# Attention and two expert layers on one core: the zero fill in three pieces, tokens counted ahead of a hidden group, half of a weight load behind a branch

## The chip, the cores and the metric

The kernel runs on one core of a Trainium2 chip. The metric is the device time of one execution in microseconds (us); the median over several runs counts. Besides, one execution is recorded by the profiler; the rows below are from that one.

## What is computed

Three stages follow one another, all in float32, here cut to what matters:

```python
scores = np.matmul(q, k.transpose(0, 1, 3, 2)) / np.sqrt(D)        # B=2, H=8, S=576, D=64
kth = np.partition(scores, -32, axis=-1)[..., -32:-31]
scores = np.where(scores >= kth, scores, -1e9)                     # the 32 largest of each row
x = softmax(scores) @ v                                            # as 1152 tokens of 512 numbers

expert_idx = np.argmax(x @ w_gate, axis=1)                         # first layer: 8 experts, one per token
...                                                                # at most 288 tokens of an expert are kept
x[i] = gate_w[i] * (relu(x[i] @ w1[e]) @ w2[e])                    # w1[e]: 512x1024, w2[e]: 1024x512
...                                                                # second layer: the same without a limit
```

## The kernel before

**Attention.** 16 heads are taken in pairs: 8 units of 9 score tiles, 72 steps in all. A tile of 128 queries by 576 keys is multiplied on TensorE (PE), its top 32 are found on VectorE (DVE) with MAX8 and MATCH_REPLACE8, ScalarE (ACT) and GpSimd (POOL) make the mask, PE transposes the masked weights and multiplies by the values. Beside the tiles there are side jobs: loads, splits, transposes of later units, writes of finished x to DRAM, and fills. A table written by hand, `at(i, f)`, says at which step a job is issued; `run_jobs` issues the jobs of a step. SyncE (SP) has no work of its own: it issues DMAs in program order and waits where one needs data.

**Fills.** `tables(zero)` returns the set-up jobs; its last five are the parts of `fill(part)` (lines 172 to 184). Parts 0 to 2 zero a third of the output each, part 3 zeroes the tails of x and y, part 4 the rows of y behind the tiles (128 rows of 9x513 words; `nov[0] + 1` is 9). The steps are in the tuple `(15, 16, 24, 33, 46)` that is zipped with them. y is the DRAM tensor between the two expert layers.

**The picked expert.** Near the end of the attention the kernel picks the expert that then has most tokens (`early_jobs`) and loads its weights as `w_early` (`w1c`, 8 loads of 512 KB, step 60). A tile of 128 of its tokens (`blank`) can so be computed before the tokens are sorted. Its hidden layer has 8 groups of 128 units; the groups f=0 and 1 are done at the end of the attention (L1029, relus in L1031), the others in `early_hidden(f)` (L1848), four float32 products each, which the profile shows as eight records. `early_out(d)` (L1857) is the second layer of this tile, four groups d of eight products (16 records).

**Two branches.** `repair(trips)` (L1069) recomputes rows whose top 32 were cut short; `spill()` (L1657, L1659) computes blocks of an expert's tokens that exceed its tiles, as many as `nblk` says. All engines load the number and branch; neither body runs here.

**Start of the first expert layer**, `begin()`: `choose` (one-hot `oh` of each token's expert, L1531, DVE), `early_hidden(2)`, `count` (L1536 to L1541, PE: positions of tokens within their expert), hidden groups 3 to 7, `spin(9, 64)` (nine products that nobody reads, L124), `ranking` (DVE), `weights(0, 0)` (both halves of the first expert's w1, L1244, on SP), `assign` (`places`, L1588, PE; `early_out(0)`; gates, `gidx`, `nblk`, DVE), gathers of token rows (`bring`, L1233, POOL), `spill`, the casts of the loaded weights (L1285 on ACT, L1286 on DVE), w2 from ACT's queue (L1256), `early_out(1)` and `(2)`, transposes of the gathered rows (L1315, PE), then the first expert's layer 1 (L1358 and on).

In `begin()` the order of the calls is the order of the instructions on each engine:

```python
choose(0, nch)
early_hidden(2)
count(0, nch)
...
early_hidden(7, 0, KD // 2)
spin(9, 64)
weave(*ranking())
weights(0, 0)
assign()
```

Of the kernel before, what the change touches and what calls it, by code (L numbers as in the profile page):

```python
# [10 lines left out]
F32 = mybir.dt.float32  # L11
# [23 lines left out]
NCOL = len(COLS[0])  # L35
FAR = 5000.0
AWAY = 2048.0
RW = 513
# [16 lines left out]
def attn_moe_moe_kernel(ctx, tc, q, k, v, g1, w11, w12, capacity, g2, w21, w22, out):  # L55
    nc = tc.nc
# [3 lines left out]
    KD = Dm // 128  # L60
    KF = F // 128
# [56 lines left out]
    part = consts.tile([128, 1], F32)  # L118
# [15 lines left out]
    def tables(zero):  # L134
        def first():
            nc.gpsimd.iota(iot, pattern=[[1, 128]], base=0, channel_multiplier=0, allow_small_or_imprecise_dtypes=True)
            nc.gpsimd.iota(part, pattern=[[0, 1]], base=0, channel_multiplier=1, allow_small_or_imprecise_dtypes=True)
            nc.gpsimd.memset(wgh, 0.0)

        def gate_in(hh):  # L140
            nc.gpsimd.tensor_copy(wgh[hh * D:(hh + 1) * D, :, hh, :], wg[hh * D:(hh + 1) * D, 0])

        def rank_tables(part):
            for t_, cols, sizes in zip(tab, COLS, SIZES):
                for a, (r, t, m) in enumerate(cols):
                    if r >= 0 and t == 0 and r // 2 == part:
                        nc.gpsimd.memset(t_[:, 0, r:r + 1], float(a + 1))
                        nc.gpsimd.memset(t_[:, 1, r:r + 1], float(sizes[r]) - AWAY)

        def clear():  # L150
            nc.gpsimd.memset(lg1, 0.0)
            nc.gpsimd.memset(lg2, 0.0)
            nc.gpsimd.memset(revm[1], 0.0)
            nc.gpsimd.memset(code[1], 0.0)

        def order():
            nc.gpsimd.tensor_scalar(chosen, negid, AWAY, 1.0, op0=OP.mult, op1=OP.mult)
            nc.gpsimd.tensor_scalar(rev, iot[:, :E], -1.0, float(E), op0=OP.mult, op1=OP.add)
            nc.gpsimd.iota(tok1, pattern=[[128, NC]], base=1, channel_multiplier=1, allow_small_or_imprecise_dtypes=True)

        def order_all():
            nc.gpsimd.tensor_copy(revm[0], rev[:, None, :].to_broadcast([128, B * NC, E]))
            nc.gpsimd.tensor_scalar(code[0][:, 0], part.to_broadcast([128, B * NC]), 1.0, 64.0, op0=OP.mult, op1=OP.add)

        def tokens(b):
            for c in range(NC):
                nc.gpsimd.memset(code[0][:, 1, b * NC + c:b * NC + c + 1], b * S + c * 128 - 64)
            t = b * NC + NC - 1
            nc.gpsimd.memset(revm[0][TAIL:, t, :], -1.0)
            nc.gpsimd.memset(code[0][TAIL:, :, t], 0.0)  # L170

        def fill(part):
            n = N // 128 // 3
            if part < 3:
                nc.sync.dma_start(out[part * n * 128:(part + 1) * n * 128].rearrange("(n p) w -> p n w", p=128),
                                  zero[:, None, :Dm].to_broadcast([128, n, Dm]))
            elif part == 3:
                nc.sync.dma_start(x_d[N:, :], zero[:128 - TAIL, :Dm])
                for a, (r, t, m) in enumerate(COLS[0]):
                    if m < 128:  # L180
                        nc.sync.dma_start(y_d[a * 128 + m:(a + 1) * 128, :], zero[:128 - m, :RW])
            else:
                nc.sync.dma_start(y_d[(NCOL - 1) * 128:, :].rearrange("(n p) w -> p n w", p=128),
                                  zero[:, None, :RW].to_broadcast([128, nov[0] + 1, RW]))

        setup_ranks.extend(lambda k=k: rank_tables(k) for k in range(4))
        return [first, lambda: gate_in(0), lambda: gate_in(1), clear, order, order_all,
                lambda: tokens(0), lambda: tokens(1)] + [lambda k=k: fill(k) for k in range(5)]

    def attention():  # L190
        HP = H // 2
# [8 lines left out]
        with tc.tile_pool(name="ald", bufs=2) as ld, tc.tile_pool(name="awk", bufs=2) as wk, \  # L200
# [644 lines left out]
                    at(i0 + NT + 6 + d, normed, u, *w)  # L845
            at(1, load, 2, ("v",))
            at(1, setup[3])
            for i, f in zip((62, 63, 64, 66, 26, 28, 30, 32), setup_ranks + setup[4:-5]):
                at(i, f)
            early_ops, weights_in, found, turn_rows = early_jobs()  # L850
            behind = []
# [4 lines left out]
            at(60, weights_in)  # L856
            at(63, found)
            at(67, turn_rows)
            for i, f in zip((15, 16, 24, 33, 46), setup[-5:]):
                at(i, f)  # L860
            at(1, lambda: nc.gpsimd.memset(flv, -1.0))
            at(0, v_first)
# [164 lines left out]
            for f, o in enumerate((rest[:, 0, :128], side[:, 0, :128])):  # L1027
# [2 lines left out]
                                     start=(d == 0), stop=(d == KD - 1))  # L1030
                relus.append(lambda f=f, o=o: nc.scalar.activation(h_early[f].bitcast(F32), o, AF.Relu))  # L1031
            relus[0]()
            g = wk.tile([128, NC, 2, E], F32, name="g")
            for c0, c1 in ((0, M - 1), (M, NC)):
                shape = [128, c1 - c0, 2, E]
# [16 lines left out]
                nc.vector.scalar_tensor_tensor(l, last[:, hh, D:D + E], r3[:, hh:hh + 1], l, op0=OP.mult, op1=OP.add)  # L1052
            b, p = divmod(u, HP)
            xn = wk.tile([128, 2, D], F32, name="xn3", bufs=1)
            for hh in range(2):
                nc.scalar.activation(xn[:, hh], last[:, hh, :D], AF.Copy, scale=r3[:, hh:hh + 1])
            relus[1]()
            nc.sync.dma_start(x_d[b * S + (M - 1) * 128:b * S + M * 128, p * 128:(p + 1) * 128],
                              xn.rearrange("s h d -> s (h d)"))
            return trips  # L1060
# [114 lines left out]
    def moe(i, pools, src, lg, w1, w2, limit):  # L1175
# [5 lines left out]
        with ExitStack():  # L1181
# [410 lines left out]
            def assign(a=0):  # L1592
# [7 lines left out]
                if i == 0:  # L1600
                    nc.scalar.activation(cnt, pos[:, nch], AF.Copy)
                    nc.scalar.activation(poss, pos[:, :nch], AF.Copy)
                    early_hidden(7, KD // 2)
                    yTs[-1] = wk.tile([128, KD, ny], F32, name="yT")
                    early_out(0, 0, KF)
                for f in gates[:3] if i == 0 else gates:
                    f()
                nc.vector.tensor_copy(lowp, pi[:, :NCOL])
# [231 lines left out]
            def early_hidden(f, d0=0, d1=KD):  # L1840
                if f == 2:
                    hTs[-1] = wt.tile([128, KF, 1, 128], F32R, name="w2c", bufs=12)
                if d0 == 0:
                    early_ps["h"] = ps.tile([128, 512], F32, name="pp", bufs=4)
                ph = early_ps["h"]
                w_, k = piece(w_early[0], f)
                for d in range(d0, d1):
                    nc.tensor.matmul(ph[:, :128], w_[:, d, k * 128:(k + 1) * 128], rows0[:, d], start=(d == 0), stop=(d == KD - 1))  # L1848
                if d1 == KD:
                    hidden(hTs[-1], f, 128, ph[:, :128], False)  # L1850
# [29 lines left out]
            def begin():  # L1880
                bank()
                choose(0, nch)
                early_hidden(2)
                count(0, nch)
                nc.scalar.activation(dl, dl, AF.Exp)
                none = new([128, 1], "none", U32)
# [1 line left out]
                yr = wk.tile([128, RW], F32, name="yr", bufs=3)  # L1888
                gather(yr[:16, :Dm], none[:16])
                two.prepare()  # L1890
                for f in range(3, 7):
                    early_hidden(f)
                early_hidden(7, 0, KD // 2)
                spin(9, 64)
                weave(*ranking())
                weights(0, 0)
                assign()
                for j in range(2):
                    bring(j)
                for f in table["later"]:  # L1900
                    f()
                spill()
                early_gate()
                for t in range(len(tiles_of(1))):
                    bring(first[1] + t)
# [3 lines left out]
                weights(0, 1, eng=ACT)  # L1909
                for f in first_split[2:4]:  # L1910
                    f()
                early_out(1, 0, KF)
                early_out(2, 0, KF)
                xTs[0] = wk.tile([128, KD, 2, MOST], F32R, name="xT")
                q0, q1 = tiles_of(0)
                rows_in(0, *q0)
# [230 lines left out]
```

## Time and profile before

| | |
|---|---|
| median of 3 runs | 584.73 us (584.01, 587.02, 584.73) |
| the profiled execution | 584.83 us, span 583.2 us, mean granted clock of PE 0.998 |
| busy share of the span | PE 97%, DVE 82%, ACT 72%, POOL 46% |
| DMA moved | 100.76 MB, mean 173 GB/s |

How to read it: the span goes from the first to the last instruction. PE is busy nearly all the time by its records, but they are pipelined and their ends are modelled; a row's duration is longer than the distance of two starts. The shares are averages over two stages, attention (to about 250 us) and expert layers (the rest), which have different limits. "Idle before" in brackets behind a row is how long the engine stood still ahead of it and what released it; "issue" means that the profile shows nothing that it waited for. An engine name with a q (SPq, PEldq) is its sequencer, which issues DMAs, waits and branches.

### The profile page before, as it was taken

The page shows a single profiled execution, that of the slowest core. Times are in us where ns is not written, and L with a number is a line of the kernel's source. Part 1 is how long each engine was busy: PE and PEld are TensorE (multiplying, and loading weights), DVE is VectorE, ACT ScalarE, POOL GpSimd, SP SyncE. Part 2 cuts the span into 40 slices and gives each one's busy share as a digit, 9 for nine tenths or more (in the row PEclk, how much of TensorE's full clock was granted, in tenths as well). Part 3 has the DMA queues.
Part 4 walks back from the last instruction along what each step waited for, and adds up shares of the span by engine and source line. Part 5 has one row for each costly group of instructions (what it writes and reads, how often), then busy time and mean ns, then how long its engine had stood idle before and what let it go on. Part 6 is the DMA issues. An engine that isn't in the chain of part 4 may idle for free.

```text
span 583.2 us, 13992 instructions
## 1 busy us (share of the span) xinstructions
PE 566.5 (97%) x4786; PEld 539.4 (92%) x4786; DVE 475.9 (82%) x1588; ACT 419.3 (72%) x1040; POOL 266.4 (46%) x600
## 2 busy tenths in 40 slices
PE   8999999999999999989999999999999999999994
PEld 5799999999998999889999999998998899999993
DVE  6999999999999999868788778552588788889650
ACT  6789998999898978627687787552365677878650
POOL 8758888988897798546320111010103302220010
PEclk9999999999999999999999999999999999999999
DMA  6630513161291083055988768876777867678650
GB/s 146 142 83 2 169 46 114 44 127 43 75 149 25 1 246 85 22 175 198 341 278 289 231 204 259 276 220 229 228 252 234 288 227 263 231 243 298 213 204 14
DMA packets 85168, 100.76 MB, mean 173 GB/s; under 512 B 33925, under 2 KB 46725, under 8 KB 85088
## 3 DMA queue, kind: packets, MB, share of 16 engines
q1 hardware_dynamic: 79104, 86.69, 49.1%
q0 software_dynamic: 3728, 10.70, 5.2%
q10 hardware_dynamic: 2256, 2.39, 1.3%
q8 instruction: 40, 0.66, 0.5%
q14 instruction: 40, 0.33, 0.2%
HBM read 86.51 MB, written 13.74 MB: 172 GB/s over the span
## 4 chain that ended last, share of the span: by engine, by line
PE 36%; DMA 10%; issue 6%; DVE 2%; POOL 1%; ACT 1%; POOLq 0%; DVEq 0%; ACTq 0%
DMA out_dram<-yr,sidx 8%; PE pp L1365 8%; PE pp L1404 7%; PE pp L1351 3%; PE pp L1367 3%; PE pp L1406 3%; PE pl L1418 2%; PE pt L1315 1%; DMA xr<-x,gidx 1%; PE pt L1455 1%; PE pp L1400 1%; PE pp L1402 1%; PE pp L1401 1%; DMA xr<-y,gid 1%; PE pp L1354 1%
## 5 line engine op out<-in xcount | busy, mean ns | idle before, releaser
L622 PE MATMUL xb<-vx,pT 128*128 128x73 f32 (+1 forms) x800 | 94.0, 266 | 0.2 <-ACT pT L1012 0.2
L1365 PE MATMUL pp<-xT,w1c 128*128 128x352 f32 (+4 forms) x316 | 92.4, 361 | 0.4 <-DVE xT L1321 0.4
L1286 DVE TENSOR_TENSOR w2c<-raw,w2c 128x512 fp32r<-128x512 f32 x112 | 74.6, 684 | 18.9 <-ACT w2c L1285 17.4
L622 PEld LDWEIGHTS xb<-vx,pT 128*128 128x128 f32 (+1 forms) x800 | 87.1, 181 | 2.5 <-issue 1.3
L1404 PE MATMUL pp<-hT,w2c 128*128 128x416 f32 (+4 forms) x320 | 88.7, 356 | 0.1
L1406 PE MATMUL pp<-hT,w2c 128*128 128x208 f32 (+4 forms) x320 | 77.8, 243 | 0.0
L1367 PE MATMUL pp<-xT,w1c 128*128 128x176 f32 (+4 forms) x316 | 77.0, 244 | 0.0
L1285 ACT ACTIVATE w2c<-raw 128x512 fp32r<-128x512 f32 x112 | 67.4, 624 | 8.8 <-DMA raw<-in_moe_w_dram 5.1
L601 PE MATMUL pt<-ident,shifted 128*128 128x128 f32 x350 | 67.4, 278 | 0.0
L602 PE MATMUL pt<-negid,under 128*128 128x128 bf16 x350 | 63.5, 219 | 0.5 <-ACT under L592 0.5
L1286 DVE TENSOR_TENSOR w1c<-raw,w1c 128x512 fp32r<-128x512 f32 x88 | 56.0, 686 | 9.3 <-ACT w1c L1285 7.4
L1337 ACT ACTIVATE t<-pp 128x208 f32<-128x208 f32 (+4 forms) x120 | 37.5, 313 | 34.5 <-PE pp L1367 21.2
L1406 PEld LDWEIGHTS pp<-hT,w2c 128*128 128x128 f32 x320 | 61.0, 191 | 0.0
L1404 PEld LDWEIGHTS pp<-hT,w2c 128*128 128x128 f32 x320 | 60.0, 188 | 1.0 <-DVE hT L1331 0.8
L1365 PEld LDWEIGHTS pp<-xT,w1c 128*128 128x128 f32 x316 | 59.4, 188 | 1.4 <-DVE xT L1321 0.8
L1367 PEld LDWEIGHTS pp<-xT,w1c 128*128 128x128 f32 x316 | 60.4, 191 | 0.0
L1467 POOL DMA_INDIRECT out_dram<-yr,sidx x14 | 13.6, 971 | 101.3 <-ACT yr L1448 84.9
L592 ACT ACTIVATE under<-s,nb 128x576 bf16<-128x576 f32 x70 | 55.0, 787 | 1.4 <-POOL nb L584 1.1
L1790 POOL DMA_DIRECT2D y<-yr x13 | 7.5, 579 | 105.4 <-issue 45.1
L521 DVE MAX8 top<-ypair 128x8 f32<-128x160 f32 x192 | 54.6, 312 | 0.0
L595 POOL TENSOR_SCALAR shifted<-s,nb 128x576 f32<-128x576 f32 x70 | 52.1, 744 | 3.9
L601 PEld LDWEIGHTS pt<-ident,shifted 128*128 128x128 f32 x350 | 49.2, 141 | 3.5
(421 smaller groups left out, 1547.3 us busy)
## 6 DMA issues: line engine op xcount, KB each, us to landing
raw<-in_moe_w_dram SPq DMA_DIRECT2D x60, 1024.0 KB, 5.3
w1c<-in_moe_w_dram SPq DMA_DIRECT2D x8, 512.0 KB, 5.9
y<-blank SPq DMA_DIRECT2D x1, 2308.5 KB
out_dram<-blank SPq DMA_DIRECT2D x3, 768.0 KB
y<-yr POOLq DMA_DIRECT2D x8, 256.5 KB
kraw<-in_k_dram SPq DMA_DIRECT2D x8, 256.0 KB
vraw<-in_v_dram SPq DMA_DIRECT2D x16, 128.0 KB, 2.9
vx<-in_v_dram SPq DMA_DIRECT2D x16, 128.0 KB, 2.9
```

Source lines behind the costliest of these rows:

```text
L521: ops.append(lambda w=w, cur=cur: nc.vector.max(w, cur))
L592: nc.scalar.activation(under[k % 3][:, :S], s, AF.Relu, bias=nb[:, 1:2], scale=-BIG)
L595: nc.gpsimd.tensor_scalar(shifted[k % 3][:, :S], s, nb[:, 0:1], 1.0, op0=OP.add, op1=OP.mult)
L601: both = (nc.tensor.matmul(pt[:, o], shifted[k % 3][:, o], ident, is_transpose=True, start=True, stop=False), nc.tensor.matmul(pt[:, o], u ...
L602: nc.tensor.matmul(pt[:, o], under[k % 3][:, o], negid, start=False, stop=True))
L622: nc.tensor.matmul(o, pT[:, c2, cols], z["v"][:, c2, hh], start=(c2 == 0), stop=(c2 == NC - 1))
L1285: nc.scalar.activation(o[:, 0], src_, AF.Copy)
L1286: nc.vector.tensor_tensor(o[:, 1], src_, o[:, 0].bitcast(F32), op=OP.subtract)
L1365: nc.tensor.matmul(ph[:, :2 * n].rearrange("p (w n) -> p w n", w=2), w[f][:, 0, d], xT[:, d, :, :n], start=st, stop=False)
L1367: nc.tensor.matmul(ph[:, :n], w[f][:, 1, d], xT[:, d, 0, :n], start=False, stop=sp)
L1404: nc.tensor.matmul(py[:, :2 * n].rearrange("p (w n) -> p w n", w=2), w[f][:, 0, o], hT[:, f, :, :n], start=st, stop=False)
L1406: nc.tensor.matmul(py[:, :n], w[f][:, 1, o], hT[:, f, 0, :n], start=False, stop=sp)
```

## The change

1. Part 4 of the fill becomes three parts of 128x3x513 words, at the steps 46, 54 and 57.
2. At the end of the attention PE issues 14 products that nobody reads (`spin(14, ...)`) ahead of the repair branch, and ACT does the relu of the hidden group 1 before the two copies xn and not after them.
3. In `begin()` `early_hidden(2)` stands after `count`. Every later hidden group moves back with it: the last 12 records of them (second half of 6, and 7) now stand where the second half of 7 and `early_out(0)` stood, `spin(9, 64)` is gone, and `early_out(0)` stands behind the overflow branch with 1 and 2.
4. The second half of the first expert's w1 is asked for on SP behind the overflow branch, with a second load of the expert's number.

```diff
@@ fill @@
             else:
-                nc.sync.dma_start(y_d[(NCOL - 1) * 128:, :].rearrange("(n p) w -> p n w", p=128),
-                                  zero[:, None, :RW].to_broadcast([128, nov[0] + 1, RW]))
+                n = nov[0] + 1
+                a, b = (part - 4) * n // 3, (part - 3) * n // 3
+                nc.sync.dma_start(y_d[(NCOL - 1 + a) * 128:(NCOL - 1 + b) * 128, :].rearrange("(n p) w -> p n w", p=128),
+                                  zero[:, None, :RW].to_broadcast([128, b - a, RW]))
...
@@ attention @@
-            for i, f in zip((15, 16, 24, 33, 46), setup[-5:]):
+            for i, f in zip((15, 16, 24, 33, 46, 54, 57), setup[-7:]):
                 at(i, f)
...
             relus[0]()
+            spin(14, rest[:, 0, :64])
...
+            relus[1]()
             for hh in range(2):
                 nc.scalar.activation(xn[:, hh], last[:, hh, :D], AF.Copy, scale=r3[:, hh:hh + 1])
-            relus[1]()
...
@@ assign @@
-                    early_hidden(7, KD // 2)
-                    yTs[-1] = wk.tile([128, KD, ny], F32, name="yT")
-                    early_out(0, 0, KF)
+                    early_hidden(6, KD // 2)
+                    early_hidden(7)
...
@@ begin @@
                 choose(0, nch)
-                early_hidden(2)
                 count(0, nch)
...
-                for f in range(3, 7):
+                for f in range(2, 6):
                     early_hidden(f)
-                early_hidden(7, 0, KD // 2)
-                spin(9, 64)
+                early_hidden(6, 0, KD // 2)
                 weave(*ranking())
-                weights(0, 0)
+                w1s[0] = [load_w1(chosen_one(0), (0,)), {}]
                 assign()
...
                 spill()
+                w1s[0][0].extend(load_w1(chosen_one(0), (1,)))
                 early_gate()
...
-                early_out(1, 0, KF)
-                early_out(2, 0, KF)
+                yTs[-1] = wk.tile([128, KD, ny], F32, name="yT")
+                for d in range(3):
+                    early_out(d, 0, KF)
```

What this does to the order of instructions is shown at three places. The first is SP's order around the fill; `x<-xn` are writes of finished tokens, `early_eid` is the number of the picked expert, whose weights are loaded behind it. Before:

```order
L655 DMA x<-xn 128x2x128 x2
L655 DMA x<-xn 64x128
L183 DMA y<-blank 128x9x513
L655 DMA x<-xn 128x2x128 x2
L655 DMA x<-xn 64x128
L388 TENSOR_LOAD early_eid
```

Now:

```order
L657 DMA x<-xn 128x2x128 x2
L657 DMA x<-xn 64x128
L185 DMA y<-blank 128x3x513
L657 DMA x<-xn 128x2x128 x2
L657 DMA x<-xn 64x128
L185 DMA y<-blank 128x3x513 x2
L390 TENSOR_LOAD early_eid
```

One third stays at the old place; two stand behind the next unit's writes of x.

The second is PE's order behind the repair branch, where `oh` is the one-hot from DVE. Before:

```order
L1069 UNCONDITIONAL_BRANCH x3
L1848 MATMUL pp<-blank,w1c 128x128 x4
L1536 LDWEIGHTS before
L1536 MATMUL pl<-oh,before 128x88
L1540 LDWEIGHTS ones
...
L1541 MATMUL pl<-oh,chosen 128x80
L1848 MATMUL pp<-blank,w1c 128x128 x18
```

Now:

```order
L1072 UNCONDITIONAL_BRANCH x3
L1539 LDWEIGHTS before
L1539 MATMUL pl<-oh,before 128x88
L1543 LDWEIGHTS ones
...
L1544 MATMUL pl<-oh,chosen 128x80
L1850 MATMUL pp<-blank,w1c 128x128 x18
```

The hidden group of four products is no longer ahead of the count; behind the count there are 18 products of hidden groups in both.

The third is PE's order ahead of the overflow branch, from the last product of the places on. Before:

```order
L1588 MATMUL pi<-r_4739,onehot 128x28
L1848 MATMUL pp<-blank,w1c 128x128 x2
L1857 MATMUL pp<-jp,w1c 128x128
L1857 MATMUL pp<-h_105,w1c 128x128
L1857 MATMUL pp<-w2c,w1c 128x128 x6
L1657 TENSOR_LOAD nblk
```

Now:

```order
L1591 MATMUL pi<-r_4755,onehot 128x28
L1850 MATMUL pp<-blank,w1c 128x128 x6
L1659 TENSOR_LOAD nblk
```

Six products stand ahead of the branch where there were ten; the eight of `early_out(0)` (L1857) have moved behind it, ahead of those of `early_out(1)` and `(2)`.

## Rows read from the trace of the kernel before

**Rows 1.** Windows: from:to, us, busy by engine (x instructions), PEclk, DMA share, GB/s.

```profile
36.00:100.00 64.00, 64.00 (x621) 61.97 (x622) 63.67 (x255) 57.36 (x142) 51.34 (x103) 1.00 0.33 93
...
180.00:200.00 20.00, 20.00 (x199) 19.35 (x200) 18.90 (x76) 18.33 (x43) 14.73 (x36) 1.00 0.06 17
...
300.00:400.00 100.00, 100.00 (x784) 97.57 (x783) 68.94 (x170) 65.96 (x169) 13.70 (x27) 1.00 0.78 249
```

**Rows 2.** Timeline of PE near 178 us: start, us, engine, line, operation, [idle before].

```profile
178.49 0.38 PE L471 MATMUL pt<-qkT 128*128 128x288 f32 x1
179.88 0.41 PE L471 MATMUL pt<-qkT 128*128 128x288 f32 x1 [1.01 <-issue]
```

**Rows 3.** Timeline of DVE, the same stretch.

```profile
181.07 0.46 DVE L503 TENSOR_TENSOR hi<-sc,s 128x288 f32<-128x288 f32 x1 [1.23 <-ACT s L476]
```

**Rows 4.** Timeline of SP's queue: DMAs issued, 65 to 210 us.

```profile
66.99 1.20 SPq L175 DMA_DIRECT2D out_dram<-blank  x1
...
158.78 0.58 SPq L183 DMA_DIRECT2D y<-blank  x1
180.06 7.85 SPq L655 DMA_DIRECT2D x<-xn  x3
205.47 2.57 SPq L399 DMA_DIRECT2D w1c<-in_moe_w_dram  x4
```

**Rows 5.** Windows of some us, around fills and at the overflow branch.

```profile
66.00:70.00 4.00, 4.00 (x42) 3.92 (x40) 4.00 (x13) 3.86 (x10) 3.11 (x7) 1.00 1.00 349
160.00:161.00 1.00, 1.00 (x13) 0.94 (x12) 0.98 (x7) 0.89 (x3) 0.92 (x3) 1.00 1.04 373
...
171.00:172.00 1.00, 1.00 (x10) 0.93 (x10) 1.00 (x6) 0.54 (x4) 1.00 (x4) 1.00 1.01 62
...
177.00:178.00 1.00, 1.00 (x11) 1.00 (x11) 1.00 (x6) 0.69 (x2) 0.89 (x3) 1.00 0.00 0
260.00:262.00 2.00, 0.48 (x4) 0.39 (x4) 0.97 (x4) 0.65 (x2) 1.81 (x6) 1.00 1.05 397
```

**Rows 6.** The page's DMA queues: packets, MB, share.

```profile
q8 instruction: 40, 0.66, 0.5%
```

**Rows 7.** Timeline of DVE, 250 to 260 us.

```profile
250.99 0.24 DVE L1531 TENSOR_TENSOR oh<-revm,m 128x80 bf16<-128x80 f32 x1
...
259.01 0.15 DVE L1632 CAST nblk<-nbf 128x1 int32<-128x1 f32 x1
```

**Rows 8.** Timeline of PE, 250 to 275 us.

```profile
251.07 1.16 PE L1848 MATMUL pp<-blank,w1c 128*128 128x128 f32 x8 [0.66 <-ACTq L1069]
252.06 0.20 PE L1536 MATMUL pl<-oh,before 128*128 128x88 bf16 x1
...
252.41 4.25 PE L1848 MATMUL pp<-blank,w1c 128*128 128x128 f32 x36
...
257.03 0.74 PE L1588 MATMUL pi<-r,onehot 128*128 128x28 bf16 x10
...
261.61 0.49 PE L1857 MATMUL pp<-jp,w1c 128*128 128x128 f32 x2 [1.52 <-ACTq L1659]
...
265.28 0.60 PE L1315 MATMUL pt<-ident,xr 128*128 128x128 f32 x4
...
274.09 0.63 PE L1315 MATMUL pt<-ident,xr 128*128 128x128 f32 x4 [0.30 <-DMA xr<-x,gidx]
```

**Rows 9.** The overflow branch by engine: durations in ns (min/median/max), first and last start.

```profile
L1659 SPq EVENT_SEMAPHORE  x9: 5/16/338, 260.1 to 263.1; - x9
...
L1659 PEldq COMPARE_BRANCH  x1: 337/337/337, 259.9 to 259.9; - x1
...
L1659 PEldq EVENT_SEMAPHORE  x1: 51/51/51, 260.6 to 260.6; - x1
...
L1659 ACTq EVENT_SEMAPHORE  x1: 17/17/17, 261.5 to 261.5; - x1
```

**Rows 10.** Timeline of ACT, 268 us.

```profile
268.20 1.66 ACT L1285 ACTIVATE w1c<-raw 128x512 fp32r<-128x512 f32 x3
```

More of the change, by code (lines that the diff above doesn't have):

```diff
@@ L182, in fill @@
             else:
-                nc.sync.dma_start(y_d[(NCOL - 1) * 128:, :].rearrange("(n p) w -> p n w", p=128),
-                                  zero[:, None, :RW].to_broadcast([128, nov[0] + 1, RW]))
+                n = nov[0] + 1
+                a, b = (part - 4) * n // 3, (part - 3) * n // 3
+                nc.sync.dma_start(y_d[(NCOL - 1 + a) * 128:(NCOL - 1 + b) * 128, :].rearrange("(n p) w -> p n w", p=128),
+                                  zero[:, None, :RW].to_broadcast([128, b - a, RW]))
         setup_ranks.extend(lambda k=k: rank_tables(k) for k in range(4))
         return [first, lambda: gate_in(0), lambda: gate_in(1), clear, order, order_all,
-                lambda: tokens(0), lambda: tokens(1)] + [lambda k=k: fill(k) for k in range(5)]
+                lambda: tokens(0), lambda: tokens(1)] + [lambda k=k: fill(k) for k in range(7)]
     def attention():
@@ L847, in attention @@
             at(1, setup[3])
-            for i, f in zip((62, 63, 64, 66, 26, 28, 30, 32), setup_ranks + setup[4:-5]):
+            for i, f in zip((62, 63, 64, 66, 26, 28, 30, 32), setup_ranks + setup[4:-7]):
                 at(i, f)
```

## The prediction

> **What bounds the kernel now.** I read the windows first. In 36 to 100 us VectorE (DVE) is busy for 63.67 of 64 us while the other engines rest here and there: DVE sets the pace of the attention. In 300 to 400 us TensorE (PE) is busy for 100.00 of 100: PE sets the pace of the experts [rows 1]. So a stop in the attention counts as DVE's lost time, and a stop after it as PE's.
>
> Then I looked for stops at the places that the diff touches. At 178.49 PE starts one 128x288 product and the next only at 179.88, 1.39 us later; 1.01 of it is idle, and the releaser is "issue": PE waits for nothing that the profile shows [rows 2]. ScalarE and DVE behind it run dry, and DVE idles for 1.23 us [rows 3]. What stands before this stop is the zero fill of y. SP issues it at 158.78 in one piece [rows 4], 128 rows of 9x513 words of 4 bytes, 2.36 MB. It starts at 373 GB/s in 160 to 161, is down at 62 in 171 to 172 with the DMA engines still wholly busy (share 1.01), and is gone in 177 to 178 [rows 5]. Instructions also come by DMA, on a queue of their own with 40 packets of 0.66 MB, 16.5 KB each [rows 6]. A piece of program that comes late behind the fill would look just so: PE stops, waits for no semaphore, and resumes shortly after the fill is through.
>
> The second place is the start of the first experts. It is a chain: DVE's one-hot "oh" is made at 250.99 to 251.23, PE counts from 252.06 because it first finishes the hidden group behind the branch (from 251.07), DVE ranks, PE places tokens from 257.03, and DVE casts nblk at 259.01 to 259.16 [rows 7, 8]. All engines then branch on nblk. PE's own branch begins at 259.9 and lasts 0.337, but ScalarE passes only at 261.5, and PE waits for it until 261.61 [rows 8, 9]. PE's next wait is 0.30 us at 274.09, for gathered rows of x [rows 8].
>
> **The change, part by part.** The sum is made against the profiled execution, 584.83 us; its span is 583.2, so 1.6 lie around it. It is 0.10 above the median of the runs, 584.73.
>
> *Fill in three.* The bytes are the same; the first third stays where it was, the other two stand back to back behind the three writes of x that begin at 180.06 and take 7.85, so at about 188 [rows 4]. Price of the stop: 1.23 us of DVE. It cannot be gained more than PE's 1.39 from start to start, and nothing is gained if the stop is not the fill's. I take **-1.2**, because the nearest rows speak for it. Two of the out fills, 768 KB each, follow one another at 65 to 70 us, the second issued at 66.99 [rows 4]: they ran at 349 GB/s in 66 to 70 and PE was busy for 4.00 of 4 us [rows 5]. PE lived from 158.78 to 178.87 before it ran out, so a burst of about 1.54 MB at 349 GB/s, an estimate of 4.4 us, is far shorter than what it has in stock. At 188 the engines are nearly idle (share 0.06 in 180 to 200) [rows 1], and the next large loads, w1c, begin at 205.47 [rows 4]. SP's value load and w1c loads stand behind the two added DMAs, about 0.6 us each by the row of one fill [rows 4], 17 us ahead of their time: 0.
>
> *Fillers and relu ahead of the repair branch.* Fourteen small products cover PE's gap before 251.07; PE waits for the branch there anyway [rows 8]. The relu goes ahead of two copies, which are still done by about the time that they were, since the relu was behind them: the branch moves by -0.1 to +0.3, and is covered by oh, which is ready only at 251.23 [rows 7]. 0.
>
> *Counting first.* PE counts from about 251.3 (oh, 251.23) instead of 252.06: everything up to nblk comes 0.76 us earlier, nblk at 258.40 [rows 7, 8]. This alone does not move the end, because PE has the same work to do; it moves what PE waits for.
>
> *PE's own work to the experts.* Count 0.35 (252.06 to 252.41), then as before 36 records of hidden groups at 4.09 (4.25 less the overlap), until 255.74; the nine fillers of old are gone. The places wait for DVE until 257.03 - 0.76 = 256.27 and take 0.6 (0.74 by their row, less the overlap). Now come the 12 records of groups 6 and 7 at 0.114 each, 1.37: 258.2. Old PE had 4 of these and 16 of early_out there, 20 in all [rows 8]. The branch then waits for nblk: as before, cast to resumption of PE's own stream is 259.9 + 0.337 + 0.37 - 259.16 = 1.44 (0.37 is the row of the branch to that of PE's semaphore, 260.6) [rows 7, 9]. That gives 259.84. ScalarE is now early: its last copy before the branch, yT, has moved behind. So PE resumes at 259.84 and not 261.61, 1.77 earlier. But it now has three groups of early_out ahead of the first transposes where it had two: the two took 265.28 - 261.61 = 3.67, three take 5.5 [rows 8]. The transposes start at 265.35: **+0.1**. Ends: -0.3 if PE resumes as the compare ends, +0.5 if ScalarE still holds it. What was gained by counting earlier is spent on the group moved behind the branch.
>
> *The gathers.* They follow nblk's chain and DVE's indices, so the awaited one goes and lands some 0.75 earlier, by 273.3. PE gets there at 274.09 - 0.30 + 0.1 = 273.9 [rows 8]. The wait of 0.30 goes: **-0.3** (0 to -0.3).
>
> *Second half of w1 behind the branch.* SP was let through the branch only at 263.1 [rows 9], with both halves asked for; it now asks for the second once it is through, with one more value load. I expect it through by about 260.5, when the first half is in: 263.1 less one half, 1.05 MB at the 397 GB/s of 260 to 262 [rows 5]. Then 3.1 MB (this half and w2) fall behind the branch; at that rate they take 7.9 us, and all are in by 268.5 at worst, this half well before. ScalarE begins to cast it only at 268.20 [rows 10]: **0**, at worst +0.5.
>
> Sum: -1.2 + 0 + 0.1 - 0.3 = -1.4: **583.4 us** for a profiled run, 1.3 under the median. All of it goes through to the end, since PE is busy without a gap afterwards.
>
> **Rule against row.** The Trainium skill says (DMA: Bandwidth & Descriptors, Queues, rings and completion order) that each DMA engine takes turns between its queues, a packet at a time; by that, a fetch of program would not stand behind a whole fill, the stop would not be the fill's, and the sum would lose its largest term. The trace neither shows nor excludes this order; it shows only a stop that begins about 2 us after the fill's last byte [rows 2, 5].
>
> **The rivals.**
> *A, the stop is not the fill's.* It comes 1 to 2 us after the fill has gone, not within it, and the profile names no cause. Then 584.83 + 0.1 - 0.3 = 584.6. For it: the delay. Against it: PE has no other stop of that form in the attention that I found, and the largest transfer lies just ahead of it.
>
> *B, slower: the stop comes more than once.* The fill's rate may fall because of its rows of 2052 bytes and not because of its size. At the whole fill's mean (2.36 MB in some 17 us, 139 GB/s) the pair of thirds takes 11 us from 188, the first third 5.5 us from 159. If a burst of that length is enough to make PE run out, there are two stops of 1.23 instead of one: 584.83 + 1.23 + 0.1 - 0.3 = 585.9. It decides once the bursts last as long as the stock of program, of which the trace only tells that it held for 19.7 us behind one issue. Against it: 373 GB/s at the start [rows 5]. The Trainium skill (DMA: Bandwidth & Descriptors, the rule under its table of sizes) asks for at least 1 MiB per DMA for 75% of the peak, and so speaks against thirds; the out fills of 768 KB at 349 GB/s do not bear it out [rows 5].
>
> *C, faster.* PE resumes at the compare's end (-0.3), and some of the 0.76 of the earlier chain shows up behind: 584.83 - 1.39 - 0.3 - 0.3 - 0.76 = 582.1.
>
> **How the numbers follow.** Forecast 0.60, its own range 582.6 to 584.3 (the ends of its terms); A 0.17, C 0.13, B 0.10. The range takes in C and B as priced, with no more than 0.3 beyond C and 0.1 beyond B: 581.8 to 586.0; what is left out are their far ends. About 0.5%, 2.9 us, is what a measurement can tell from no change: faster is under 581.8, slower above 587.6. The forecast lies wholly within it, as do A and B as priced; C's lower half and a little of the forecast's tail reach below (0.10), and B with a longer second stop reaches above (0.03).
>
> **What would show it.** Right: no idle of PE by "issue" at the 128x288 product near 178, DVE without a stop there; the pair of thirds near 188 at above 300 GB/s; PE counting at about 250 (251.3 less 1.2), resuming behind the overflow branch 1.77 earlier against the attention's end, and the first transposes at the old distance; no wait for gathered rows at 273. Wrong: the same stop with a third of the fill ahead of it (A), a second stop between 190 and 205 (B), PE waiting for w1c or its casts near 273, or ScalarE still last at the branch.

## The result and the profile after

| | before | the change |
|---|---|---|
| median of 8 runs | 584.49 us (583.81 to 587.66) | 589.65 us (588.05 to 592.63) |
| profiled execution, span | 584.83, 583.2 | 588.05, 586.4 |
| mean granted clock of PE | 0.998 | 0.994 |

The ratio is 1.0088, 95% interval 1.0065 to 1.0111: the change is slower by 0.9%, where 583.4 and a range of 581.8 to 586.0 were forecast. Beside the kernel before on two other occasions the ratio was 1.0084 both times. The lines of the changed kernel are two or three further on than those of before (L471 is now L473, L1857 L1859).

**The attention went as forecast.** Timeline of PE, changed kernel, where the stop was [rows 2]:

```profile
178.34 0.51 PE L473 MATMUL pt<-qkT 128*128 128x288 f32 x2
```

Two products in one row with no idle time ahead of them: the stop is gone. The one-hot of the experts' start is made 1.39 us earlier, at 249.60 where it was 250.99 [rows 7]. The pair of thirds, asked for from 186.54 on, moved more slowly than I thought. Windows of the changed kernel (columns as in [rows 1]):

```profile
186.00:190.00 4.00, 4.00 (x47) 3.86 (x44) 4.00 (x14) 3.71 (x10) 3.26 (x9) 1.00 0.64 225
190.00:194.00 4.00, 4.00 (x41) 3.94 (x41) 3.98 (x18) 3.38 (x9) 2.12 (x7) 1.00 1.09 124
```

The first of these windows is only partly filled (share 0.64): from 188 to 190 the pair ran at 369 and 363 GB/s, from 190 to 192 at 152 and 125 with the DMA engines still busy, and it was through at about 196. PE is busy for 4.00 of 4 us all the same. The first third, at 159, was through by 162.

**The start of the experts went as forecast, up to 272 us.** Timeline of PE and two rows of DVE, changed kernel:

```profile
249.99 0.20 PE L1539 MATMUL pl<-oh,before 128*128 128x88 bf16 x1 [0.57 <-DVE oh L1534]
...
258.28 0.46 PE L1859 MATMUL pp<-jp,w1c 128*128 128x128 f32 x2 [1.21 <-ACT w2c L1336]
...
263.71 0.60 PE L1318 MATMUL pt<-ident,xr 128*128 128x128 f32 x4
...
272.36 0.63 PE L1318 MATMUL pt<-ident,xr 128*128 128x128 f32 x4
274.93 0.46 PE L1368 MATMUL pp<-xT,w1c 128*128 128x416 f32 x1 [1.95 <-DVE s L1341]
...
275.32 0.37 PE L1368 MATMUL pp<-xT,w1c 128*128 128x416 f32 x1
...
275.62 0.37 PE L1368 MATMUL pp<-xT,w1c 128*128 128x416 f32 x1
...
277.86 0.59 PE L1368 MATMUL pp<-xT,w1c 128*128 128x416 f32 x1
...
278.42 0.59 PE L1368 MATMUL pp<-xT,w1c 128*128 128x416 f32 x1
...
279.47 0.97 PE L1421 MATMUL pl<-wg,yT 128*128 128x8 f32 x8
```

```profile
249.60 0.24 DVE L1534 TENSOR_TENSOR oh<-revm,m 128x80 bf16<-128x80 f32 x1
...
274.51 0.37 DVE L1341 TENSOR_TENSOR s<-pp,t 128x208 f32<-128x208 f32 x1
```

Counted from the end of oh (251.23 before, 249.84 now), PE resumes behind the overflow branch after 8.44 us and not 10.38, starts the first transposes after 13.87 and not 14.05, and the third after 22.52 and not 22.86, without waiting for gathered rows [rows 8]. Then comes what was not there before: PE waits 1.95 us at 274.93. It waits until DVE has emptied a product bank, the memory that PE writes its products into (274.51), and on DVE this stands behind casts of w1. From there PE is slower too: 275.32 and 275.62 are 0.30 apart, two products of the same form at 277.86 and 278.42 are 0.56 apart. ScalarE's timeline and the piece of the chain of waits that belongs to it tell why:

```profile
259.15 0.40 ACTq L1259 DMA_DIRECT2D raw<-in_moe_w_dram  x1
...
259.73 0.59 ACTq L1259 DMA_DIRECT2D raw<-in_moe_w_dram  x1
...
272.03 1.67 ACT L1288 ACTIVATE w1c<-raw 128x512 fp32r<-128x512 f32 x3 [5.30 <-DMA raw<-in_moe_w_dram]
```

```profile
259.92 12.09 DMA raw<-in_moe_w_dram
```

The second half of w1, asked for on SP at 259.92, lands 12.09 us later; ScalarE stands still for 5.30 us before its cast, which began at 268.20 in the kernel before [rows 10]. ScalarE had asked for the two halves of w2 at 259.15 and 259.73, ahead of it. Windows of the changed kernel:

```profile
262.00:270.00 8.00, 8.00 (x74) 7.90 (x74) 2.13 (x4) 1.87 (x5) 4.07 (x7) 1.00 1.00 370
272.00:274.00 2.00, 0.84 (x6) 0.42 (x4) 1.30 (x3) 1.97 (x5) 0.00 (x0) 1.00 0.01 2
276.00:278.00 2.00, 2.00 (x10) 1.55 (x10) 1.90 (x8) 1.55 (x6) 1.83 (x6) 0.50 0.00 0
278.00:280.00 2.00, 2.00 (x13) 1.95 (x12) 2.00 (x7) 2.00 (x6) 1.55 (x6) 0.66 0.00 0
```

From 262 to 270 the DMA engines are wholly busy (share 1.00 at 370 GB/s). Then PE is busy for 0.84 of 2 us, and behind that its granted clock is 0.50 and 0.66, the lower of its two levels (1.2 and 2.4 GHz) for most of 4 us.

What the DMA engines move in that time is told by the queues of the changed kernel in 264 to 269 us (packets, MB, share of 16 engines; q10 carries ScalarE's requests, q1 SP's):

```profile
q10 hardware_dynamic: 440, 0.89, 49.5%
q1 hardware_dynamic: 430, 0.87, 47.2%
```

While both move, the half and w2 get about the same. The half loses its time ahead of that: its first bytes move at 263.2, 3.3 us after its request, while the first bytes of w2 had moved at 260.2, 1.1 us after theirs, and 0.77 MB of w2 were in by 263. Between 269 and 271 two gathers of token rows take 0.36 MB more ahead of its end.

### The profile page after: what moved, and what is told of

Read it like the earlier page. It is cut to its first block, busy times and chain, and to the rows that moved or that the text cites. A ratio compares the mean times of both kernels' runs of the same rounds, so it can differ in the third digit from the quotient of the medians.

```text
span 586.4 us, 14001 instructions
## 1 busy us (share of the span) xinstructions
PE 568.3 (97%) x4791; PEld 540.7 (92%) x4791; DVE 475.7 (81%) x1588; ACT 419.8 (72%) x1040; POOL 266.9 (46%) x600
## 4 chain that ended last, share of the span: by engine, by line
PE 34%; DMA 11%; issue 5%; DVE 3%; ACT 1%; POOLq 0%; POOL 0%; SPq 0%; DVEq 0%; ACTq 0%
DMA out_dram<-yr,sidx 8%; PE pp L1407 7%; PE pp L1368 7%; PE pp L1354 3%; PE pp L1409 3%; PE pp L1370 3%; DMA raw<-in_moe_w_dram 2%; PE pl L1421 1%; PE pt L1318 1%; PE pt L1458 1%; PE pp L1403 1%; PE pp L1405 1%; PE pp L1404 1%; DVE w2c L1289 1%; DMA xr<-y,gid 1%
## 5 line engine op out<-in xcount | busy, mean ns | idle before, releaser
L1368 PE MATMUL pp<-xT,w1c 128*128 128x352 f32 (+4 forms) x316 | 93.7, 364 | 2.4 <-DVE s L1341 1.9
L1288 ACT ACTIVATE w1c<-raw 128x512 fp32r<-128x512 f32 x88 | 49.4, 621 | 7.2 <-DMA raw<-in_moe_w_dram 5.3
```

Source lines behind the costliest of these rows:

```text
L1288: nc.scalar.activation(o[:, 0], src_, AF.Copy)
L1368: nc.tensor.matmul(ph[:, :2 * n].rearrange("p (w n) -> p w n", w=2), w[f][:, 0, d], xT[:, d, :, :n], start=st, stop=False)
```

## The experiments

All times are medians; "before" is the kernel before, run beside each on the same chip. Chips differ by some us, so only ratios are compared across rows.

| run | us | before | ratio, 95% interval |
|---|---|---|---|
| e1 fill in three alone | 584.53 | 586.14 | 0.9960, 0.9935 to 0.9985 |
| e2 change without the late half | 584.49 | 586.14 | 0.9961, 0.9940 to 0.9981 |
| e3 late half alone | 585.81 | 586.14 | 0.9982, 0.9954 to 1.0009 |
| e4 w2 behind the half, on SP | 584.28 | 586.14 | 0.9958, 0.9934 to 0.9981 |
| e5 the change again | 591.45 | 585.25 | 1.0084, 1.0046 to 1.0122 |
| e6 w2 requests two casts later | 591.38 | 585.25 | 1.0086, 1.0055 to 1.0117 |
| e7 late casts behind an emptying | 589.82 | 585.25 | 1.0070, 1.0049 to 1.0092 |
| e8 thirds in a burst | 584.81 | 585.25 | 0.9988, 0.9969 to 1.0007 |
| e9 w2 behind an output copy | 582.69 | 583.39 | 0.9973, 0.9951 to 0.9995 |
| e10 w2 first, half last, on SP | 590.16 | 583.39 | 1.0101, 1.0058 to 1.0145 |
| e12 filled wait | 590.45 | 583.39 | 1.0088, 1.0053 to 1.0124 |
| e13 whole fill at step 54 | 582.86 | 583.39 | 0.9987, 0.9967 to 1.0007 |
| e14 filled wait, free bank | 586.48 | 583.03 | 1.0058, 1.0014 to 1.0102 |
| e15 the change beside e14 | 587.08 | 583.03 | 1.0084, 1.0054 to 1.0113 |

### Which part costs it: e1 to e4

The fill alone, on the kernel before:

```diff
-                nc.sync.dma_start(y_d[(NCOL - 1) * 128:, :]...
+                ...three parts, as in the change, at steps 46, 54, 57
```

> The kernel before with the fill in three pieces alone. If the stop of PE near 178 us is the single fill's, it goes and the time falls by 1.2 to 1.4, from 584.5 to about 583.2, with nothing else moved. If the stop has another cause, it stays and the time is 584.5.

1.6 us less: the stop goes (the product that stood still near 178 starts at 178.44 without idle time), and with it the long end of the times, 583.69 to 585.54 where before had 584.75 to 590.98.

The change without its late half:

```diff
-                w1s[0] = [load_w1(chosen_one(0), (0,)), {}]
+                weights(0, 0)
...
-                w1s[0][0].extend(load_w1(chosen_one(0), (1,)))
```

> The change without its last part: both halves of w1 are asked for ahead of the overflow branch, as before. Theory 1, the late half costs all of it: the late cast near 272 goes, the clock stays full, and the time is 582.7 (584.5 less 1.4 of the fill and 0.4 of the start of the experts). Theory 2, the moved products of PE or the fillers cost it: the time stays above 586.

Theory 1: the whole loss goes. Beyond the fill alone (e1) it gains nothing that shows (584.49 and 584.53).

The late half alone, on the kernel before:

```diff
-                weights(0, 0)
+                w1s[0] = [load_w1(chosen_one(0), (0,)), {}]
...
                 spill()
+                w1s[0][0].extend(load_w1(chosen_one(0), (1,)))
```

> The kernel before with the second half of w1 asked for behind the overflow branch, and nothing else. Theory 1: ScalarE waits for the half until about 272, PE waits and loses clock as in the change, and the time is 588 to 590. Theory 2: the load lands in time and the time is 584.5.

Here theory 1 missed: the late half alone costs nothing (ratio 0.9982). The requests for `raw`, first and last start, and ScalarE's cast, in this run:

```profile
L1256 ACTq DMA_DIRECT2D raw<-in_moe_w_dram x2: 389/394/398, 265.5 to 266.1; - x2
...
L1244 SPq DMA_DIRECT2D raw<-in_moe_w_dram x1: 394/394/394, 265.3 to 265.3; - x1
```

```profile
272.39 1.68 ACT L1285 ACTIVATE w1c<-raw 128x512 fp32r<-128x512 f32 x3 [0.76 <-DMA raw<-in_moe_w_dram]
```

With early_out(0) and its copy still ahead of the branch, ScalarE comes out of it behind SP: the half is asked for at 265.3, w2 at 265.5 and 266.1. It lands within 7.1 us, and ScalarE waits 0.76. So neither part alone is to blame: the moved copy lets ScalarE's w2 requests overtake the half that was moved behind the branch. In the trace of this run w2's first bytes move at 268.3, and the half has the DMA engines to itself from 266.3 until then.

w2 behind the half, both on SP:

```diff
-                weights(0, 1, eng=ACT)
+                weights(0, 1)
```

> The change with w2 of the first expert asked for on SP behind the second half of w1, and not on ScalarE's queue ahead of it. Theory 1a, the half is late because 2 MB of w2 share the DMA engines with it: it lands some 5 us after it is asked for near 260, is cast by 268, and the time is about 583. Theory 1b, asking behind the branch is itself too late: the half still lands at 268 or later and the time stays above 586.

Requests, ScalarE's cast and PE in this run:

```profile
L1259 SPq DMA_DIRECT2D raw<-in_moe_w_dram x2: 373/373/373, 260.7 to 261.3; - x2
...
L1247 SPq DMA_DIRECT2D raw<-in_moe_w_dram x1: 394/394/394, 259.8 to 259.8; - x1
```

```profile
266.54 1.66 ACT L1288 ACTIVATE w1c<-raw 128x512 fp32r<-128x512 f32 x3
```

```profile
258.19 0.46 PE L1859 MATMUL pp<-jp,w1c 128*128 128x128 f32 x2 [1.25 <-ACT w2c L1336]
...
272.32 0.43 PE L1368 MATMUL pp<-xT,w1c 128*128 128x416 f32 x1
...
275.36 0.97 PE L1421 MATMUL pl<-wg,yT 128*128 128x8 f32 x8
```

Theory 1a. The half is asked for at 259.8, as late as in the change, and the cast starts at 266.54 without a wait. Asking behind the branch is not itself too late; what stands ahead of the half is. PE's rows give the bill: it resumes at 258.19 (258.28 in the change), reaches the product of 274.93 at 272.32, 2.61 us earlier, and the row L1421 at 275.36 and not 279.47, 4.11 earlier. So 2.6 of the 5.1 between the two profiled executions (588.05 and 582.92) are the wait, 1.5 the lower clock behind it (PE does not idle in that stretch), and the rest comes later. The two were not run beside each other, but they differ by only 0.09 where PE resumes. In medians the late half costs more: the ratio of the change is 1.0084 on this chip (e5, below) and 0.9961 without its late half (e2), which makes 1.2%, some 7 us.

### Is it the order of the requests: e5, e6, e9, e10

> The change itself once more, beside the others on one chip. If the loss belongs to the kernel and not to the chip of the first comparison: 3 to 5 us above the kernel before, and some 5 us above the change with w2 behind the half.

The loss is the kernel's, not a chip's. By the medians it is 6.2 us, more than the 3 to 5 expected, and the times range from 588.69 (mean clock 0.993) to 593.42 (0.986).

```diff
-                for f in first_split[:2]:
+                for f in first_split[:4]:
                     f()
                 weights(0, 1, eng=ACT)
-                for f in first_split[2:4]:
-                    f()
```

> The change with ScalarE's two w2 requests behind four casts of w1 and not behind two, so some 1.2 us later and after SP's request of the half near 260; nothing else moves. Theory 1a, order of the requests: the half then goes ahead of w2, lands by 266 to 268, and the time falls by 4 to 5, to that of the kernel with w2 behind the half. Theory 1c, any sharing with 2 MB of w2 makes the half late, whoever asks first: the half lands at 270 or later and at most 1 us is gained.

It missed its aim. ScalarE's timeline in this run:

```profile
259.09 0.40 ACTq L1259 DMA_DIRECT2D raw<-in_moe_w_dram  x1
...
259.67 0.71 ACTq L1259 DMA_DIRECT2D raw<-in_moe_w_dram  x1
260.15 0.61 ACT L1288 ACTIVATE w1c<-raw 128x512 fp32r<-128x512 f32 x1
```

The requests stand behind four casts in the program, and yet they go out at 259.09 and 259.67, before the fourth cast has begun (260.15). Nothing moved, so nothing could be told of the order. It does show how far the price ranges: PE waits 2.08 us at 275.13, and behind that its granted clock is 0.50 in every window from 278 to 286, some 10 us with the parts at both ends, where the profiled execution of the change had some 3.4.

```diff
-                weights(0, 1, eng=ACT)
...
                 for d in range(3):
                     early_out(d, 0, KF)
+                    if d == 0:
+                        weights(0, 1, eng=ACT)
```

> The change with ScalarE's w2 requests behind four casts and the first copy of early_out, which waits for PE until about 260.1; so they come after SP's request of the half, still on the other queue. Theory 1a, the order of the requests decides, across queues too: the half lands by 268, no wait of PE near 274, and the time falls by 4 to 5, below the kernel before. Theory 1c, two queues share whatever the order: the half lands at 270 or later and at most 1.5 come back.

Now a copy that waits for PE holds them. Requests and cast in this run:

```profile
L1247 SPq DMA_DIRECT2D raw<-in_moe_w_dram x1: 393/393/393, 259.2 to 259.2; - x1
```

```profile
260.89 0.97 ACTq L1259 DMA_DIRECT2D raw<-in_moe_w_dram  x2
...
266.68 1.67 ACT L1288 ACTIVATE w1c<-raw 128x512 fp32r<-128x512 f32 x3
```

Half at 259.2, w2 from 260.89 on the other queue, cast at 266.68 without a wait. Theory 1a, and with 582.69 a kernel that is faster than the one before too (ratio 0.9973, barely clear of 1).

```diff
-                w1s[0][0].extend(load_w1(chosen_one(0), (1,)))
+                weights(0, 1)
+                w1s[0][0].extend(load_w1(chosen_one(0), (1,)))
...
-                weights(0, 1, eng=ACT)
```

> The change with all three requests on SP behind the branch, w2 first and the half of w1 last: the reverse of the kernel with w2 behind the half, with nothing on ScalarE's queue. Theory 1a: the half lands 10 us or more after it is asked for, and the time is that of the change or above, 589 to 592. If the second queue were to blame, it would be 584 to 585.

Slower again, 590.16, with one queue only. The chain's piece of the half and two windows behind PE's wait:

```profile
261.32 11.77 DMA raw<-in_moe_w_dram
```

```profile
276.00:278.00 2.00, 1.99 (x7) 1.95 (x8) 1.90 (x6) 2.00 (x7) 1.81 (x5) 0.50 0.00 0
280.00:284.00 4.00, 4.00 (x18) 3.93 (x17) 4.00 (x11) 3.36 (x9) 0.63 (x4) 0.50 0.41 91
```

12 us from request to landing, and then PE at half clock. e4 and e10 differ in the order of three requests alone, and by 1.4% of the time in their ratios: the order decides, on one queue as on two. What it decides on two queues is when a load's first bytes move: in e9 w2 on ScalarE's queue begins 2.6 us after its request, behind the half, which began after 1.1.

### What the lateness does to PE: e7, e12, e14, e15

```diff
-                for f in first_split[4:7]:
-                    f()
-                table["left"] = first_split[7:]
+                table["left"] = first_split[4:]
```

> The change with the casts of the late half behind the first emptying of a product bank on ScalarE and VectorE, and not ahead of it; the half still lands near 272. Theory 2a, PE stops because the emptying of its banks is queued behind casts that wait for the half: PE's wait shrinks from 1.95 to under 0.8, the clock stays full, and 3 to 4 us come back. Theory 2b, PE stops because it needs the half itself: at most 1 us comes back.

ScalarE's timeline and PE's waits (total, times, longest) in this run:

```profile
267.87 0.34 ACT L1340 ACTIVATE t<-pp 128x208 f32<-128x208 f32 x1 [1.05 <-PE pp L1365]
273.60 2.19 ACT L1288 ACTIVATE w1c<-raw 128x512 fp32r<-128x512 f32 x4 [5.38 <-DMA raw<-in_moe_w_dram]
```

```profile
PE pp L1368 <- DVE s L1341: 1.0, 1, 1.0
PE pp L1368 <- ACT w1c L1288: 0.9, 1, 0.9
```

The first bank is emptied at 267.87, ahead of the late casts; but PE now waits 0.9 for the cast and 1.0 for the next emptying, 1.9 in all. This is nearer to theory 2b: PE needs the half itself at that place, and the order of casts and emptyings mostly chose which row the wait stands on. By the medians 1.6 us came back (589.82 and 591.45 in e5), between the two forecasts, but the intervals of the two ratios overlap.

```diff
+                    def busy():
+                        o = ps.tile([128, KD, 128], F32, name="pt")
+                        for _ in range(80):
+                            idle_product(o[:, 0, :64])
```

> The change with 80 small products that nobody reads ahead of PE's wait for the emptied bank near 272, some 2.3 us of them, so that PE does not fall idle there. If the lower clock after the wait (0.50 in 276 to 278, 0.66 in 278 to 280) is a loss of its own, it stays at 1.00 and some 1.5 us come back. If not, the time is that of the change.

```profile
279.28 0.46 PE L1318 MATMUL pt<-ident,xr 64*128 64x64 f32 x4 [2.97 <-DVE raw L1245]
```

The filler ran for 2.50 us from 272.55, and then (timeline of PE) later transposes waited 2.97. The row names a DVE instruction (raw, L1245) as what ended the wait; that the bank taken by the filler caused it is an inference, from e14, where the filler has another bank and no such wait stands. The times went from 584.98 to 592.75, with one of 595.27. It tells nothing of the clock.

```diff
-                        o = ps.tile([128, KD, 128], F32, name="pt")
-                        for _ in range(80):
-                            idle_product(o[:, 0, :64])
+                        o = ps.tile([128, 512], F32, name="pl", bufs=1)
+                        for _ in range(100):
+                            idle_product(o[:, :64])
```

> The change with 100 small products that nobody reads, some 3.1 us of them, ahead of PE's wait near 272, into a bank that is free then (80 of them in a bank that the next transposes need had put a wait of 2.97 us in its place). If the lower clock after the wait is a loss of its own, it stays at 1.00 in 274 to 284 and the time is 1.5 us or more below the change beside it, with less spread. If the late half alone sets the time, it is that of the change, up to 1 us more where the wait is shorter than the fill.

> The change itself, beside the filled wait on one chip: 3 to 6 us above the kernel before, with a lower clock (0.50 to 0.66) for some us after PE's wait near 272 to 276.

Inconclusive: 586.48 and 587.08 lie within each other's range, and the granted clock stays at 1.00 from 270 to 290 in both profiled executions, so the loss that the filler was to take away was not there. The half was less late here: SP asked for it at 259.02, between the two requests of w2 (258.84 and 259.42), and its first bytes moved after 1.8 us and not 3.3. ScalarE's cast and PE's later waits in the change itself (e15):

```profile
269.78 1.68 ACT L1288 ACTIVATE w1c<-raw 128x512 fp32r<-128x512 f32 x3 [3.18 <-DMA raw<-in_moe_w_dram]
```

```profile
282.43 0.46 PE L1407 MATMUL pp<-hT,w2c 128*128 128x416 f32 x1 [0.75 <-DVE hT L1334]
...
283.64 0.46 PE L1407 MATMUL pp<-hT,w2c 128*128 128x416 f32 x1 [0.65 <-DVE hT L1334]
```

The cast starts at 269.78; PE does not stop at 274 and keeps its clock, and yet it waits at 282 and 283 for hidden groups that ScalarE and DVE, now behind with their casts, deliver late (e4 has no such waits, the change has one of 0.67 at 285.89). The lateness is paid in another place. What the lower clock costs by itself stays with the rows (1.5 us in the profiled execution of the change); no run here took it away alone.

### What makes the stop near 178: e8, e13

```diff
-            for i, f in zip((15, 16, 24, 33, 46, 54, 57), setup[-7:]):
+            for i, f in zip((15, 16, 24, 33, 46, 46, 46), setup[-7:]):
```

> The kernel before with the fill in three requests, all three at step 46 back to back. If the size of a burst makes PE stop, the stop near 178 stays and the time is that of the kernel before. If the single request is what does it, the stop goes and the time is that of the fill in three alone, 1.2 to 1.6 less.

The stop goes, though the rate falls as it did for the one request [rows 5]. The time that was to go with it hardly shows: 0.4 us less than before and not 1.2 to 1.6, and the interval takes in no difference. Windows of this run:

```profile
160.00:162.00 2.00, 2.00 (x22) 1.94 (x21) 1.98 (x10) 1.89 (x4) 1.92 (x3) 1.00 1.02 377
168.00:170.00 2.00, 2.00 (x22) 1.88 (x21) 2.00 (x6) 2.00 (x8) 1.90 (x6) 1.00 1.07 97
```

Times of 583.74 to 585.21; before had 584.02 to 591.54.

```diff
-            for i, f in zip((15, 16, 24, 33, 46), setup[-5:]):
+            for i, f in zip((15, 16, 24, 33, 54), setup[-5:]):
```

> The kernel before with its whole fill at step 54 and not 46, so that SP asks for it near 188 and not 159. If PE's stop belongs to the single fill, it moves along, to about 205 to 209, and the time is that of the kernel before or, with the loads of w1c behind it, up to 1 us more. If it belongs to that place of the program, it stays near 178.

Neither came: the stop is at no place. SP's request and a window late in the fill:

```profile
186.49 0.58 SPq L183 DMA_DIRECT2D y<-blank  x1
```

```profile
198.00:202.00 4.00, 4.00 (x40) 3.79 (x39) 4.00 (x15) 3.80 (x13) 3.19 (x8) 1.00 0.57 53
```

The whole fill in one request is still under way at 198 to 202, at 53 GB/s, and PE is busy for 4.00 of 4 us; the times are 582.54 to 583.40. So, as far as one profiled execution of each tells, it takes the single request and that place of the program together.

The packets of the instruction queue [rows 6] tell more. In the 13 profiled executions with at most a third of the fill near 159, a packet of 16 KB moves at 164.3 to 165.1 and takes 0.9 to 1.5 us. In the two with the stop (before and e3) none moves between 153.5 and 175; then one starts at 175.28 and 175.77, takes 3.1 and 3.3 us and is through at 178.38 and 179.07, close to PE's stop (178.87 to 179.88 in before). In e8 it starts at 173.57 and is through at 175.90, and in e13, with the fill at 186, a packet starts at 197.63 that starts at 190.03 in e8; PE stops in neither. So a piece of program does come some 11 us late behind the single fill, as the prediction guessed. That PE waited for this piece stands in no row; it fits the times.

What the stop costs differs from run to run. The profiled execution of e3, which has the old fill, shows it (timeline of PE, then windows):

```profile
179.94 0.40 PE L471 MATMUL pt<-qkT 128*128 128x288 f32 x1 [1.20 <-issue]
```

```profile
180.00:182.00 2.00, 2.00 (x16) 1.87 (x16) 0.88 (x3) 1.55 (x4) 0.88 (x4) 0.76 0.25 70
182.00:184.00 2.00, 2.00 (x12) 2.00 (x12) 2.00 (x6) 0.97 (x3) 0.95 (x2) 0.50 0.03 4
184.00:186.00 2.00, 2.00 (x12) 1.86 (x12) 2.00 (x11) 1.54 (x4) 1.90 (x3) 0.50 0.00 0
186.00:188.00 2.00, 2.00 (x13) 1.81 (x12) 1.52 (x9) 1.25 (x2) 1.74 (x5) 0.54 0.23 70
```

The stop is 1.20 us, hardly more than the 1.01 of [rows 2], but here the granted clock falls behind it: 0.50 to 0.76 in the windows from 180 to 188, which makes some 7 us at the lower level. In [rows 1] it stayed at 1.00. This fits that the kernel before ranges so widely (584.02 to 591.54 beside e8) and e1, e8, e9 and e13, without the stop, do not.

## Why the prediction was wrong

- **The fill: right.** -1.2 was forecast, -1.39 is what the start of the experts moved, and the fill alone is worth 0.4% (0.15% to 0.65%, e1). In e8 and e13, where the stop is gone by other means, the medians are only 0.4 and 0.5 us lower and the intervals take in no difference, so the gain in the times is less sure than the stop itself. Its guess at the cause, a piece of program late behind the fill, has the late packet for it, which the trace of the kernel before already held, though the prediction says that the trace neither shows nor excludes it. Two of its reasons were not: the pair of thirds ran at above 349 GB/s for its first 2 us only, and the three thirds in a burst, or the whole fill at another place, do not stop PE (e8, e13). Rival B was right that the rate falls within the pair (which took some 8.5 us where B had 11), wrong for the first third (some 3 us where B had 5.5), and wrong in the consequence.
- **Counting first, PE's path, the gathers: right in size.** +0.1 was forecast for the first transposes and, with the -0.3 of the gathers, -0.2 for the third; the trace has -0.18 and -0.34 from the end of oh. In the times (e2 against e1) it does not show.
- **The clock: no term.** The prediction put nothing for it. The granted clock stays at 1.00 through the branch and falls only behind PE's wait.
- **"Second half of w1 behind the branch": this step failed.** I wrote that SP would be through at about 260.5, that 3.1 MB fall behind the branch, "and all are in by 268.5 at worst, this half well before", cost 0, at most +0.5. SP was through at 259.9, earlier than that. But the half did not come "well before" the rest: it landed at 272.0, where the last bytes of w2 moved at 272.1. I had noted in the step before that ScalarE is early at the branch now because its copy moved behind it, and did not ask what else ScalarE would do earlier. It asked for w2, 0.8 and 0.2 us ahead of SP, so w2 moved alone until 263.2 and then shared the DMA engines with the half. The bytes were also too few: besides the 3.1 MB two gathers of token rows, some 0.4 MB, fall in ahead of the half's end.
- **The price of being late: too small.** I allowed 0.5. It was 1.95 of waiting, about 1.5 of lower clock behind the wait, and later waits for hidden groups, 5.1 in all between the profiled executions of the change and e4, and some 7 in the medians. None of the rivals had it; my note on what would prove me wrong ("PE waiting for w1c or its casts near 273") named the place.

The Trainium skill (DMA: Bandwidth & Descriptors, Queues, rings and completion order) says that a DMA engine takes turns between its queues. By that, if it held from the request on, the half on SP's queue would share evenly with w2 on ScalarE's and land once some 2.1 MB had moved, an estimate of 5.7 us at 370 GB/s, ahead of its cast. The trace agrees where both move (0.87 and 0.89 MB in 264 to 269), but not for the whole 12.09 us: the half's first bytes came 3.3 us after its request. Why they came so late is not shown; the DMA engines were not full then (share 0.50 in 260 to 261).

## What to carry to other kernels

Where a change takes work off an engine ahead of a branch or a wait, follow everything that this engine issues behind it, its DMA requests first: what it now asks for earlier can go ahead of what another engine asks for. A load that is moved later is to be priced by all requests that stand ahead of it at that moment, not by its own bytes. And a wait of PE of about two us may cost as much again in clock, or more: about 1.5 us behind 1.95 in the change, and some 10 us at half clock behind 2.08 in e6.

## What the runs showed of the hardware that was not expected

- The order of requests changes how long a large load takes even on different queues: 7.1 us for the half when it was asked for 0.2 us ahead of w2 (e3), 12.1 when 0.2 to 0.8 us behind (the change). The load asked for first moved its first bytes 1.0 to 1.1 us after its request (e3, e9, the change), one asked for behind another 1.8 to 3.7 us after it (e15, e9, e3, the change, e5). Once both moved, they got about the same.
- Writes of 2052-byte rows began at 373 and 377 GB/s and slowed down while they went on: to 121 after 6 us and 62 after 11 in one request (before), to 188 after 2 us and 97 after 8 in three asked for together (e8). A third by itself was through before that (the change).
- A request that stands behind four casts in ScalarE's program left before the fourth cast began (e6); behind a copy that waits for PE it left only at 260.89 (e9).
- A stop of PE of 1.01 us left the granted clock at 1.00 in one execution (before), and one of 1.20 us was followed by some 7 us at the lower level in another (e3).
